# 384 rows of w4 moved to partitions 0 to 63 in eight-partition loads, and w3's products taken block by block

## The chip, the cores and the metric

The kernel runs on one core of a Trainium2 chip. The time is the device time of one execution in microseconds (us); the number that counts is the median of the runs, 197.53 us before the change.

## What is computed

One decode step (sequence length 1) of a small transformer block for a batch of 8 and a width D = 512, all in bf16:

```
A(x):  q = x @ wq  (32 heads of 128)                 k, v: the last 2048 positions of the caches (8 kv heads)
       softmax(q k^T / sqrt(128)) v, heads joined, @ wo
B(x):  x1 = x + hs          (the token shift is zero for a sequence of 1, so hs = 0)
       x1 + gelu(layernorm(x1) @ w3) @ w4            w3: 512 x 1792, w4: 1792 x 512
h   = x + A(layernorm(x))
out = h + B(layernorm(h))
```

The caches are the bulk of the work: 16 units of K and 16 of V of 2 MB each, against 4 MB each of `wq` and `wo` and 1.8 MB each of `w3` and `w4`.

## The kernel before

**Order and queues.** The program is written as five lists, one for each engine (`PE`, `AC`, `DV`, `PO`, `SP`; class `Engine`, line 47). Each entry names the semaphores that it waits for, and each engine works through its list in order. Nearly every transfer is issued by SyncE (`dma`, line 187), so all loads go through one queue, in the order in which they were written: `wq`, then K and V units as their buffers come free, `wo` in pieces, and last `w3` and `w4`. A load's semaphore rises by 16 in all as the DMA engines that carry it finish; a wait for 16 is a wait for the whole load.

**Attention.** For each K unit (lines 461 to 502) TensorE turns 128x128 blocks over (line 267), ScalarE and VectorE copy the result out (lines 273 and 275), and TensorE forms the scores (line 291). One softmax is done per batch row. V units follow three units later (line 372). The V unit that comes last is loaded in four pieces (line 415), and the last half of `wo` in four single groups (lines 513 and 514).

**The end, around the change.** TensorE multiplies the attention output by `wo` (line 433) into `hT_ps`, features on partitions and batch in the columns. VectorE takes the mean (lines 534 to 541, with a small TensorE product in line 537); `hb` (line 538) is the centred input to `w3`. A second small product (line 558) gives the variance; ScalarE takes the root (lines 559 and 560), VectorE the reciprocals (561, 562) and the residual `fin` (564).

`w3` (line 519) is loaded into the buffer of K unit 12 in four loads of 128 rows, under one semaphore. `w4` (lines 520 to 526) goes into the buffer of K unit 13 in four loads over all 128 partitions: three of 512 rows with four rows per partition (`w4_a`; 4 KB a partition) and one of 256 rows with two rows per partition (2 KB a partition). A chunk is what one product of `w4` contracts, 128 rows, one from each partition; there are FC = 14. Since a partition holds rows 4p to 4p+3 of its load, the matching columns of `w3` are picked with a stride of 4, or of 2 in the last load (`w3_cols`, line 546).

`pe_w3` (line 551) goes over the chunks and, in each, over the four blocks of 128 rows of `w3`, so each 128x8 result is finished before the next begins; it is called twice, for seven chunks each, and the first call waits for all of `w3` (line 565). Each half is scaled by VectorE (line 570) and put through the gelu by ScalarE (line 572). `pe_w4` (line 579) then adds the 14 chunks into one tile `z_ps`, with waits for the gelu halves and for the loads: the first waits for two loads of `w4` (`sem_w4a`), the others for `sem_w4b` and `sem_w4c`. Line 587 adds the residual, line 590 turns the result, line 591 copies it and line 594 stores it.

Of the kernel before, what the change touches and what calls it, by code (L numbers as in the profile page):

```python
# [7 lines left out]
ACT = mybir.ActivationFunctionType  # L8
ALU = mybir.AluOpType
AX = mybir.AxisListType  # L10

B = 8
D = 512
# [6 lines left out]
W0 = SK - W  # L20
NC = W // 128
F = 1792
FC = F // 128
KC = D // 128
EPS = 1e-5
GELU_C = math.sqrt(2.0 / math.pi)
# [4 lines left out]
U = 4  # L31
# [4 lines left out]
NK = 4  # L36
# [40 lines left out]
def bass_sequential_preLN__sliding_block_cached__mixer_s_mlp__decode_kernel(  # L77
# [19 lines left out]
    NUN = NB * NU  # L97
# [4 lines left out]
    with es:  # L102
        sb = lambda shape, dtype, name: es.enter_context(nc.sbuf_tensor(name, shape, dtype))
        ps_t = lambda shape, dtype, name: es.enter_context(nc.psum_tensor(name, shape, dtype))
        S = lambda name: es.enter_context(nc.semaphore(name))

        knat = sb([128, NK, UL], dt.bfloat16, "knat")
# [2 lines left out]
        wq_v = wbig[:, :].rearrange("p (k n) -> p k n", k=KC)  # L110
        wo_v = wbig[:, :].rearrange("p (g k n) -> p g k n", g=G, k=R)
        w3_sb = knat[:, 0, 0:KC * F].rearrange("p (k f) -> p k f", k=KC)
        w4_sb = knat[:, 1, 0:FC * D].rearrange("p (c n) -> p c n", c=FC)

        ident_f = sb([128, 128], dt.float32, "ident_f")
        ident_b = sb([128, 128], dt.bfloat16, "ident_b")
# [39 lines left out]
        at = [0]  # L156

        def tl(n, bf=False):
            t = tail[:, at[0]:at[0] + n]
            at[0] += n  # L160
            return t.bitcast(dt.bfloat16) if bf else t
        hs, hc, hsq, xb, fin = (tl(NH) for _ in range(5))
        hsum, vsum = tl(B), tl(B)
        vv, rr = tl(2 * B), tl(2 * B)
        g_x = tl(FC * B)
        hb, gT, fT = tl(NH // 2, True), tl(FC * B // 2, True), tl(NH // 2, True)
        out_sb = sb([NH, 128], dt.bfloat16, "out_sb")

        kT_ps = [ps_t([128, W], dt.bfloat16, f"kT_ps{i}") for i in range(2)]
        kbank = [kT_ps[i // 2][:, (i % 2) * 1024:(i % 2 + 1) * 1024].bitcast(dt.float32) for i in range(4)]  # L170
# [9 lines left out]
        sem_v = [S(f"sem_v{i}") for i in range(NV)]  # L180
        sem_vl = [S(f"sem_vl{i}") for i in range(U)]
        sem_wl = [S(f"sem_wl{i}") for i in range(2)]
        sem_x, sem_wq, sem_wo, sem_w3, sem_w4a, sem_w4b, sem_w4c, sem_out = (
            S(n) for n in ("sem_x", "sem_wq", "sem_wo", "sem_w3", "sem_w4a", "sem_w4b", "sem_w4c", "sem_out"))
        PE, AC, DV, PO, SP = (Engine(S(n)) for n in ("s_pe", "s_act", "s_dve", "s_pool", "s_sp"))

        def dma(eng, dst, src, sem, *waits):
            def f(e):
                e.dma_start(dst, src).then_inc(sem, 16)  # L189
            eng.op(f, *waits, inc=False)  # L190
# [16 lines left out]
        e = DV.op(lambda e: e.bn_stats(st6[:, :], x_sb[:, :]), X)  # L207
        e = DV.op(lambda e: e.bn_aggr(mv[:, :], st6[:, :]), e)
        e = AC.op(lambda e: e.activation(rstd[:, :], mv[:, 1:2], ACT.Sqrt, bias=eps1[0:B, :], scale=1.0), e, e_eps)
        e = DV.op(lambda e: e.reciprocal(rstd[:, :], rstd[:, :]), e)  # L210
# [24 lines left out]
        e = PE.op(pe_xT, e_xln, e_idb)  # L235
# [20 lines left out]
        e_T, e_Tlo, e_Thi, e_lo, e_hi, e_QK, e_PV = {}, [], [], [], [], {}, {}  # L256
        e_ev, e_Pz = {}, {}
        e_max, e_mT, e_neg, e_negps, e_negc, e_exp, e_PT, e_pS, e_lsel, e_Lb, e_rL, e_scale, e_sc = ({} for _ in range(13))
# [202 lines left out]
        for n in range(NUN):  # L461
# [8 lines left out]
            i = U * n  # L470
# [45 lines left out]
        e_gl = AC.op(lambda e: e.activation(scratch[:, 1:2], scratch[:, 0:1], ACT.Sqrt), e_warm)  # L516

        for k in range(KC):
            dma(SP, w3_sb[:, k, :], B_w3[128 * k:128 * (k + 1), :], sem_w3, e_T[U * (NUN - NK + 1) - 1])
        FA = 12  # L520
        w4_a = B_w4[0:FA * 128, :].rearrange("(a p c) n -> p a (c n)", p=128, c=4)
        for a, sem in ((0, sem_w4a), (1, sem_w4a), (2, sem_w4b)):
            dma(SP, w4_sb[:, 4 * a:4 * a + 4, :].rearrange("p c n -> p (c n)"), w4_a[:, a, :], sem,
                e_T[U * (NUN - NK + 2) - 1])
        dma(SP, w4_sb[:, FA:FC, :].rearrange("p c n -> p (c n)"),
            B_w4[FA * 128:F, :].rearrange("(p c) n -> p (c n)", c=FC - FA), sem_w4c)

        v3 = lambda t: t.rearrange("p (n b) -> p n b", b=B)
        vr = lambda t: t.rearrange("p (n b) -> p b n", b=B)

        def bc(a, k=KC):
            return bass.AP(tensor=a.tensor, offset=a.offset, ap=[a.ap[0], [0, k], [1, B]])
# [5 lines left out]
        e_hb = DV.op(lambda e: e.tensor_tensor(v3(hb[:, :]), v3(hs[:, :]), bc(st1), ALU.add), e_mu, e_hs)  # L538
        e = DV.op(lambda e: e.tensor_tensor(v3(hc[:, :]), v3(hs[:, :]), bc(st1), ALU.add))
        e = DV.op(lambda e: e.tensor_tensor(hsq[:, :], hc[:, :], hc[:, :], ALU.mult), e)  # L540
        e_vs = DV.op(lambda e: e.tensor_reduce(vsum[:, :], vr(hsq[:, :]), AX.X, ALU.add), e)

        y_ps = [kbank[0], kbank[2]]
        FH = FC // 2

        def w3_cols(kc, f):
            a, c = divmod(f, 4)
            s = 4 if a < 3 else 2
            return w3_sb[:, kc, 512 * a + c:512 * a + c + 127 * s + 1:s]

        def pe_w3(e, n, f0, f1):
            for f in range(f0, f1):
                for kc in range(KC):
                    ins = e.matmul(y_ps[n][:, f * B:(f + 1) * B], w3_cols(kc, n * FH + f),
                                   hb[:, kc * B:(kc + 1) * B], start=(kc == 0), stop=(kc == KC - 1))
            return ins

        e = PE.op(lambda e: e.matmul(st2, ones_v[:, :], vsum[:, :], start=True, stop=True), e_vs, e_sc[NUN - 1])  # L558
        e2 = AC.op(lambda e: e.activation(vv[:, 0:B], st2, ACT.Sqrt, bias=eps2[:, :], scale=1.0 + EPS), e)  # L559
        e1 = AC.op(lambda e: e.activation(vv[:, B:2 * B], st2, ACT.Sqrt, bias=eps1[:, :], scale=1.0))  # L560
        e_rr = DV.op(lambda e: e.reciprocal(rr[:, 0:B], vv[:, 0:B]), e2)
        e_r1 = DV.op(lambda e: e.reciprocal(rr[:, B:2 * B], vv[:, B:2 * B]), e1)
        e = DV.op(lambda e: e.tensor_tensor(v3(xb[:, :]), v3(hc[:, :]), bc(rr[:, B:2 * B]), ALU.mult), e_r1)
        e_fin = DV.op(lambda e: e.tensor_tensor(fin[:, :], hs[:, :], xb[:, :], ALU.add), e)
        e_y = [PE.op(lambda e: pe_w3(e, 0, 0, FH), e_hb, (sem_w3, 16 * KC), e_lo[-1], e_hi[-1], e_lo[-2], e_hi[-2]),
               PE.op(lambda e: pe_w3(e, 1, 0, FH))]
        e_gT = []
        for n in range(2):
            cs = slice(n * FH * B, (n + 1) * FH * B)
            e = DV.op(lambda e, n=n, cs=cs: e.tensor_tensor(v3(g_x[:, cs]), v3(y_ps[n][:, 0:FH * B]),  # L570
                                                            bc(rr[:, 0:B], FH), ALU.mult), e_y[n], e_rr)
            e_gT.append(AC.op(lambda e, cs=cs: e.activation(gT[:, cs], g_x[:, cs], ACT.Gelu_apprx_tanh), e))

        z_ps = S_ps[1]
        for lo, hi, waits in ((0, FH, (e_gT[0], e_exp[NB - 1], (sem_w4a, 32))),
                              (FH, 8, (e_gT[1],)),
                              (8, FA, ((sem_w4b, 16),)),
                              (FA, FC, ((sem_w4c, 16),))):
            def pe_w4(e, lo=lo, hi=hi):
                for fc in range(lo, hi):  # L580
                    for nb in range(KC):
                        ins = e.matmul(z_ps[:, nb * B:(nb + 1) * B], w4_sb[:, fc, nb * 128:(nb + 1) * 128],
                                       gT[:, fc * B:(fc + 1) * B], start=(fc == 0 and nb == 0),
                                       stop=(fc == FC - 1), skip_group_check=True)
                return ins
            e_z = PE.op(pe_w4, *waits)
        e = DV.op(lambda e: e.tensor_tensor(fT[:, :].rearrange("p (b n) -> p n b", n=KC), v3(fin[:, :]),
                                            v3(z_ps[:, 0:NH]), ALU.add), e_z, e_fin)
        o_ps = sm[0:NH, 64:128].bitcast(dt.bfloat16)
        e = PE.op(lambda e: e.matmul(o_ps, fT[:, :], ident_b[:, :], is_transpose=True), e)  # L590
# [40 lines left out]
```

## Time and profile before

| | |
|---|---|
| median of 3 runs | 197.53 us (197.46 to 197.57) |
| the profiled execution | 197.9 us, its span 196.5 us, so 1.4 us around the span |
| mean granted TensorE clock | 0.862 over the span; 0.50 in every stretch from 170 us on |
| busy share of the span | PE 81%, PEld 66%, DVE 51%, ACT 44%, POOL 2% |
| HBM read | 79.18 MB, 403 GB/s over the span |
| packets of the program's DMA queue | 96.0% of sixteen DMA engines' span; packets of kind "instruction" on a queue of their own: 23, 0.38 MB, 0.8% |

All times below are counted from the first instruction of the span. The trace holds one execution; its sum is therefore made against 197.9 us, which is 0.37 us above the median. Beside the instructions the trace has a record of every DMA packet (start, length, size and queue, but not which of the sixteen engines carried it) and of every step of a load's semaphore.

### The profile page before, as it was taken

The numbers are of one execution on the slowest core, as the hardware profiler recorded it, in microseconds if no ns is written. First come the engines' busy times: TensorE is split into PE (matmuls) and PEld (weight loads), VectorE is DVE, ScalarE is ACT, GpSimd is POOL, SyncE is SP. The second block draws the span as 40 slices with busy tenths as digits, with TensorE's granted clock in tenths as the row PEclk, the third lists the DMA queues.
The fourth block names the chain that finished last, engine by engine and source line by source line (L and its number), as shares of the span: only waits on it lengthen the run. The fifth ranks groups of instructions, "written<-read, shape, count | busy, mean of one in ns | idle before, by whom it ended". The sixth has DMA issues, their size and how long they took to land.

```text
span 196.5 us, 6336 instructions
## 1 busy us (share of the span) xinstructions
PE 159.3 (81%) x2925; PEld 130.0 (66%) x2925; DVE 100.0 (51%) x227; ACT 87.1 (44%) x100; POOL 4.4 (2%) x12
## 2 busy tenths in 40 slices
PE   0027986989998999999987699999999898887564
PEld 0027863766877677867765668697868585787463
DVE  7401445875484557558544375547554954720041
ACT  5000565864545454637453255545453673140030
POOL 8000000000000000000000000000000000000000
PEclk9999999999699969999999589957996998555555
DMA  6999999999999999999999999999999999999961
GB/s 228 440 417 430 434 430 434 427 425 420 420 419 425 424 424 424 420 429 427 417 420 427 424 427 427 430 424 427 427 424 429 420 424 427 400 408 406 408 269 42
DMA packets 7546, 79.59 MB, mean 405 GB/s; under 512 B 856, under 2 KB 864, under 8 KB 3424
## 3 DMA queue, kind: packets, MB, share of 16 engines
q1 hardware_dynamic: 7504, 79.18, 96.0%
q8 instruction: 23, 0.38, 0.8%
q14 instruction: 3, 0.02, 0.0%
q10 hardware_dynamic: 16, 0.01, 0.0%
HBM read 79.18 MB, written 0.01 MB: 403 GB/s over the span
## 4 chain that ended last, share of the span: by engine, by line
PE 46%; DMA 33%; DVE 13%; SPq 6%; issue 2%
PE kT_ps L267 30%; DMA knat<-in_A_k_cache_dram 26%; DMA knat<-in_B_w_dram 8%; PE S_ps L291 7%; SPq L189 6%; DVE kT_sb L275 5%; PE oT_ps L372 4%; DVE mcol L302 2%; DVE Pz L336 2%; PE sm L317 1%; PE sm L306 1%; DVE Mrow L308 1%; DVE rLk L356 1%; DVE rL L350 1%; DVE negrow L313 1%
## 5 line engine op out<-in xcount | busy, mean ns | idle before, releaser
L273 ACT ACTIVATE kT_sb<-kT_ps 128x1024 bf16<-128x1024 bf16 x64 | 65.0, 1023 | 48.2 <-PE kT_ps L267 47.7
L267 PE MATMUL kT_ps<-perm_k,knat 128*128 128x128 bf16 x1024 | 77.9, 238 | 4.0 <-DMA knat<-in_A_k_cache_dram 2.8
L267 PEld LDWEIGHTS kT_ps<-perm_k,knat 128*128 128x128 bf16 x1024 | 67.6, 108 | 11.5 <-issue 8.3
L275 DVE COPY kT_sb<-kT_ps 128x1024 bf16<-128x1024 bf16 x64 | 44.2, 690 | 38.4 <-PE kT_ps L267 38.2
L372 PEld LDWEIGHTS oT_ps<-pS,vnat 128*128 128x128 bf16 x1024 | 29.7, 98 | 8.3 <-issue 7.5
L372 PE MATMUL oT_ps<-pS,vnat 128*128 128x16 bf16 x1024 | 33.6, 171 | 2.0 <-DVE oK L382 0.9
L291 PE MATMUL S_ps<-kT_sb,qz 128*32 128x512 bf16 x256 | 26.5, 402 | 4.7 <-DVE kT_sb L275 4.2
L336 DVE TENSOR_TENSOR Pz<-P_sb,mJ 128x512 bf16<-128x512 bf16 x32 | 21.6, 682 | 0.0
L323 ACT ACTIVATE P_sb<-S_ps,negcol 128x512 bf16<-128x512 f32 x8 | 5.5, 687 | 23.4 <-DVE negcol L320 23.4
L291 PEld LDWEIGHTS S_ps<-kT_sb,qz 128*32 128x32 bf16 x256 | 7.1, 93 | 12.1 <-ACT kT_sb L273 4.1
L273 ACT ACTIVATE pS<-kT_ps 128x1024 bf16<-128x1024 bf16 x8 | 8.2, 1023 | 14.9 <-PE kT_ps L267 14.9
L275 DVE COPY pS<-kT_ps 128x1024 bf16<-128x1024 bf16 x8 | 5.5, 691 | 7.9 <-PE kT_ps L267 7.9
L382 DVE TENSOR_TENSOR oK<-oT_ps,rLk 128x64 bf16<-128x64 f32 x16 | 3.6, 224 | 11.4 <-PE oT_ps L372 11.4
L267 PE MATMUL kT_ps<-perm_p,Pz 128*128 128x128 bf16 x128 | 9.4, 231 | 0.0
L267 PEld LDWEIGHTS kT_ps<-perm_p,Pz 128*128 128x128 bf16 x128 | 8.1, 105 | 1.6 <-issue 1.6
L243 PE MATMUL S_ps<-xlnT,wbig 128*128 128x8 bf16 x128 | 3.6, 168 | 6.7 <-DMA wbig<-in_A_wq_dram 6.7
L243 PEld LDWEIGHTS S_ps<-xlnT,wbig 128*128 128x128 bf16 x128 | 3.5, 104 | 6.8 <-issue 6.8
L302 DVE TENSOR_REDUCE mcol<-S_ps 128x1 f32<-128x512 f32 x8 | 5.5, 691 | 4.8 <-PE S_ps L291 4.8
L559 ACT ACTIVATE Pz<-oT_ps,eps 128x8 f32<-128x8 f32 x1 | 0.3, 267 | 15.2 <-PE oT_ps L558 15.2
L250 DVE TENSOR_SCALAR qz<-S_ps 128x32 bf16<-128x32 f32 x8 | 0.9, 181 | 9.3 <-PE S_ps L243 9.3
L433 PE MATMUL S_ps<-o,wbig 128*128 128x8 bf16 x128 | 3.9, 168 | 2.1 <-issue 1.7
L231 PE MATMUL sm<-ident_b,xln_b 8*128 8x8 bf16 x4 | 0.3, 175 | 6.3 <-DVE xln_b L211 6.3
(78 smaller groups left out, 77.9 us busy)
## 6 DMA issues: line engine op xcount, KB each, us to landing
knat<-in_A_k_cache_dram SPq DMA_DIRECT2D x16, 2048.0 KB, 29.6
vnat<-in_A_v_cache_dram SPq DMA_DIRECT2D x15, 2048.0 KB, 31.8
wbig<-in_A_wq_dram SPq DMA_DIRECT2D x1, 4096.0 KB, 12.5
wbig<-in_A_wo_dram SPq DMA_DIRECT2D x2, 1024.0 KB, 31.6
vnat<-in_A_v_cache_dram SPq DMA_DIRECT2D x4, 512.0 KB, 10.3
wbig<-in_A_wo_dram SPq DMA_DIRECT2D x4, 512.0 KB, 11.2
knat<-in_B_w_dram SPq DMA_DIRECT2D x4, 448.0 KB, 12.5
knat<-in_B_w_dram SPq DMA_DIRECT2D x3, 512.0 KB, 14.5
```

Source lines behind the costliest of these rows:

```text
L189: e.dma_start(dst, src).then_inc(sem, 16)
L243: ins = e.matmul(S_ps[0][:, h * B:(h + 1) * B], wq_v[:, kc, h * DH:(h + 1) * DH], xlnT[:, kc * B:(kc + 1) * B], start=(kc == 0), stop=(kc ...
L267: ins = e.matmul(kT_ps[k % 2][:, c * 128:(c + 1) * 128], src[:, c * DH:(c + 1) * DH], perm[:, :], is_transpose=True)
L273: e_lo.append(AC.op(lambda e: e.activation(dst[:, 0:1024], kT_ps[k % 2][:, 0:1024], ACT.Copy), e_Tlo[k], *free))
L275: e_hi.append(DV.op(lambda e: e.tensor_copy(dst[:, 1024:2048], kT_ps[k % 2][:, 1024:2048]), e_Thi[k], *free))
L291: ins = e.matmul(S_ps[b % 2][32 * j:32 * (j + 1), :].rearrange("p (c r) -> p c r", c=16), qz[:, b, J * t + j, lo:lo + 32], kT_sb[:, i % NK ...
L302: e_max[b] = DV.op(lambda e: e.tensor_reduce(mcol[:, :], S_ps[b % 2][:, :], AX.X, ALU.max), e_QK[NU * U * (b + 1) - 1], e_mT.get(b - 1))
L323: e_exp[b] = AC.op(lambda e: e.activation(P_sb[:, :], S_ps[s][:, :], ACT.Exp, bias=negcol[:, s:s + 1], scale=1.0, accum_out=lcol[:, s:s + 1]),
L336: e_Pz[b, part] = DV.op(lambda e: e.tensor_tensor(Pz[:, 0, J * w * part:J * w * (part + 1)].rearrange("p (x j) -> p x j", j=J), p_bc, m_bc ...
L372: ins = e.matmul(dst, vnat[:, n % NV, (16 * w + c) * DH:(16 * w + c + 1) * DH], mvg, start=(w == 0 and c == 0), stop=(w == U - 1 and c == 15),
L382: e_sc[n] = DV.op(lambda e: e.tensor_tensor(oK[:, n % 2].rearrange("p g r k -> p (g r) k"), s_bc, rLk[:, b % 2, 16 * t:16 * t + 16, :], AL ...
L433: ins = e.matmul(hT_ps[:, nb * B:(nb + 1) * B], wo_v[:, g, k, nb * 128:(nb + 1) * 128], o2[:, g, k, :], start=False, stop=(g == G - 1 and ...
```

## The change

- `w4` has 11 chunks of 128 rows (FCM) and six chunks of 64 rows (FX), 17 in all. The last 384 rows lie six per partition on partitions 0 to 63 (`w4x_sb`), in the buffer of K unit 14. They come in eight loads of eight partitions each; the partitions of one load lie four apart, and each holds 6 KB. These eight loads stand in SyncE's queue between `w3` and the rest of `w4`.
- The other 1408 rows come in three loads over 128 partitions: two of 512 rows (four per partition), each now with a semaphore of its own, and one of 384 rows (three per partition).
- Each block of 128 rows of `w3` has a semaphore of its own. TensorE takes the blocks in the outer loop and all 17 chunks in the inner one, so a block's products wait for that block alone, and all results are finished in the last block. The results lie in three PSUM banks: six chunks of 64 rows, eight of 128, three of 128.
- The scaling and the gelu run in three parts, in that order, and so do the products with `w4`: the 64-row chunks first, then the others. There are 68 products with `w3` and 68 with `w4`; before there were 56 and 56.

```diff
-FC = F // 128
+FX = 6
+FCM = (F - 64 * FX) // 128
+FA = 8
+FC = FCM + FX
+FX0 = FCM * 128
...
+        w4x_sb = knat[0:64, 2, 0:FX * D].rearrange("p (c n) -> p c n", c=FX)
...
         for k in range(KC):
-            dma(SP, w3_sb[:, k, :], B_w3[128 * k:128 * (k + 1), :], sem_w3, e_T[U * (NUN - NK + 1) - 1])
-        FA = 12
+            dma(SP, w3_sb[:, k, :], B_w3[128 * k:128 * (k + 1), :], sem_w3[k], e_T[U * (NUN - NK + 1) - 1])
+        w4_x = B_w4[FX0:F, :].rearrange("(h a i c) n -> h i a (c n)", h=2, a=8, c=FX)
+        for h in range(2):
+            for i in range(4):
+                dma(SP, w4x_sb[32 * h + i:32 * h + i + 29:4, :, :].rearrange("p c n -> p (c n)"), w4_x[h, i], sem_w4x,
+                    e_T[U * (NUN - NK + 3) - 1])
...
-        for a, sem in ((0, sem_w4a), (1, sem_w4a), (2, sem_w4b)):
-            dma(SP, w4_sb[:, 4 * a:4 * a + 4, :].rearrange("p c n -> p (c n)"), w4_a[:, a, :], sem,
-                e_T[U * (NUN - NK + 2) - 1])
-        dma(SP, w4_sb[:, FA:FC, :].rearrange("p c n -> p (c n)"),
-            B_w4[FA * 128:F, :].rearrange("(p c) n -> p (c n)", c=FC - FA), sem_w4c)
+        for a in range(FA // 4):
+            dma(SP, w4_sb[:, 4 * a:4 * a + 4, :].rearrange("p c n -> p (c n)"), w4_a[:, a, :], sem_w4a[a], w4_free)
+        dma(SP, w4_sb[:, FA:FCM, :].rearrange("p c n -> p (c n)"),
+            B_w4[FA * 128:FX0, :].rearrange("(p c) n -> p (c n)", c=FCM - FA), sem_w4b)
...
+        parts = ((FCM, FC, 64, kbank[1]), (0, FA, 128, kbank[0]), (FA, FCM, 128, kbank[2]))
...
+        def pe_w3(e, kc, f0, f1, m, y):
             for f in range(f0, f1):
-                for kc in range(KC):
-                    ins = e.matmul(y_ps[n][:, f * B:(f + 1) * B], w3_cols(kc, n * FH + f),
-                                   hb[:, kc * B:(kc + 1) * B], start=(kc == 0), stop=(kc == KC - 1))
+                ins = e.matmul(y[0:m, (f - f0) * B:(f - f0 + 1) * B], w3_cols(kc, f), hb[:, kc * B:(kc + 1) * B],
+                               start=(kc == 0 and f == f0), stop=(kc == KC - 1), skip_group_check=True)
...
+        for kc in range(KC):
+            e_y = [PE.op(lambda e, kc=kc, p=p: pe_w3(e, kc, *p), e_hb, (sem_w3[kc], 16), *y_free) for p in parts]
...
+        for f0, f1, n, waits in ((FCM, FC, 0, ((sem_w4x, 128), e_exp[NB - 2])), (0, 4, 1, ((sem_w4a[0], 16),)),
+                                 (4, FA, 1, ((sem_w4a[1], 16),)), (FA, FCM, 2, ((sem_w4b, 16),))):
```

More of the change, by code (lines that the diff above doesn't have):

```diff
@@ L112, in bass_sequential_preLN__sliding_block_cached__mixer_s_mlp__decode_kernel @@
         w3_sb = knat[:, 0, 0:KC * F].rearrange("p (k f) -> p k f", k=KC)
-        w4_sb = knat[:, 1, 0:FC * D].rearrange("p (c n) -> p c n", c=FC)
+        w4_sb = knat[:, 1, 0:FCM * D].rearrange("p (c n) -> p c n", c=FCM)
+        w4x_sb = knat[0:64, 2, 0:FX * D].rearrange("p (c n) -> p c n", c=FX)
         ident_f = sb([128, 128], dt.float32, "ident_f")
@@ L182, in bass_sequential_preLN__sliding_block_cached__mixer_s_mlp__decode_kernel @@
         sem_wl = [S(f"sem_wl{i}") for i in range(2)]
-        sem_x, sem_wq, sem_wo, sem_w3, sem_w4a, sem_w4b, sem_w4c, sem_out = (
-            S(n) for n in ("sem_x", "sem_wq", "sem_wo", "sem_w3", "sem_w4a", "sem_w4b", "sem_w4c", "sem_out"))
+        sem_w3 = [S(f"sem_w3{i}") for i in range(KC)]
+        sem_w4a = [S(f"sem_w4a{i}") for i in range(2)]
+        sem_x, sem_wq, sem_wo, sem_w4b, sem_w4x, sem_out = (
+            S(n) for n in ("sem_x", "sem_wq", "sem_wo", "sem_w4b", "sem_w4x", "sem_out"))
         PE, AC, DV, PO, SP = (Engine(S(n)) for n in ("s_pe", "s_act", "s_dve", "s_pool", "s_sp"))
@@ L518, in bass_sequential_preLN__sliding_block_cached__mixer_s_mlp__decode_kernel @@
         for k in range(KC):
-            dma(SP, w3_sb[:, k, :], B_w3[128 * k:128 * (k + 1), :], sem_w3, e_T[U * (NUN - NK + 1) - 1])
-        FA = 12
-        w4_a = B_w4[0:FA * 128, :].rearrange("(a p c) n -> p a (c n)", p=128, c=4)
-        for a, sem in ((0, sem_w4a), (1, sem_w4a), (2, sem_w4b)):
-            dma(SP, w4_sb[:, 4 * a:4 * a + 4, :].rearrange("p c n -> p (c n)"), w4_a[:, a, :], sem,
-                e_T[U * (NUN - NK + 2) - 1])
-        dma(SP, w4_sb[:, FA:FC, :].rearrange("p c n -> p (c n)"),
-            B_w4[FA * 128:F, :].rearrange("(p c) n -> p (c n)", c=FC - FA), sem_w4c)
+            dma(SP, w3_sb[:, k, :], B_w3[128 * k:128 * (k + 1), :], sem_w3[k], e_T[U * (NUN - NK + 1) - 1])
[4 more added lines that the diff above has]
+                    e_T[U * (NUN - NK + 3) - 1])
+        w4_free = e_T[U * (NUN - NK + 2) - 1]
+        w4_a = B_w4[0:FA * 128, :].rearrange("(a p c) n -> p a (c n)", p=128, c=4)
+        for a in range(FA // 4):
+            dma(SP, w4_sb[:, 4 * a:4 * a + 4, :].rearrange("p c n -> p (c n)"), w4_a[:, a, :], sem_w4a[a], w4_free)
+        dma(SP, w4_sb[:, FA:FCM, :].rearrange("p c n -> p (c n)"),
+            B_w4[FA * 128:FX0, :].rearrange("(p c) n -> p (c n)", c=FCM - FA), sem_w4b)
         v3 = lambda t: t.rearrange("p (n b) -> p n b", b=B)
@@ L541, in bass_sequential_preLN__sliding_block_cached__mixer_s_mlp__decode_kernel @@
         e_vs = DV.op(lambda e: e.tensor_reduce(vsum[:, :], vr(hsq[:, :]), AX.X, ALU.add), e)
-        y_ps = [kbank[0], kbank[2]]
-        FH = FC // 2
+        parts = ((FCM, FC, 64, kbank[1]), (0, FA, 128, kbank[0]), (FA, FCM, 128, kbank[2]))
         def w3_cols(kc, f):
[L547 to L551, printed above, removed]
+            if f >= FCM:
+                at, st, m = FX0 + f - FCM, FX, 64
+            elif f >= FA:
+                at, st, m = FA * 128 + f - FA, FCM - FA, 128
+            else:
+                at, st, m = 512 * (f // 4) + f % 4, 4, 128
+            return w3_sb[:, kc, at:at + (m - 1) * st + 1:st]
+        def pe_w3(e, kc, f0, f1, m, y):
             for f in range(f0, f1):
-                for kc in range(KC):
-                    ins = e.matmul(y_ps[n][:, f * B:(f + 1) * B], w3_cols(kc, n * FH + f),
-                                   hb[:, kc * B:(kc + 1) * B], start=(kc == 0), stop=(kc == KC - 1))
+                ins = e.matmul(y[0:m, (f - f0) * B:(f - f0 + 1) * B], w3_cols(kc, f), hb[:, kc * B:(kc + 1) * B],
+                               start=(kc == 0 and f == f0), stop=(kc == KC - 1), skip_group_check=True)
             return ins
@@ L564, in bass_sequential_preLN__sliding_block_cached__mixer_s_mlp__decode_kernel @@
         e_fin = DV.op(lambda e: e.tensor_tensor(fin[:, :], hs[:, :], xb[:, :], ALU.add), e)
-        e_y = [PE.op(lambda e: pe_w3(e, 0, 0, FH), e_hb, (sem_w3, 16 * KC), e_lo[-1], e_hi[-1], e_lo[-2], e_hi[-2]),
-               PE.op(lambda e: pe_w3(e, 1, 0, FH))]
+        y_free = (e_lo[-1], e_hi[-1], e_lo[-2], e_hi[-2])
+        for kc in range(KC):
+            e_y = [PE.op(lambda e, kc=kc, p=p: pe_w3(e, kc, *p), e_hb, (sem_w3[kc], 16), *y_free) for p in parts]
         e_gT = []
[L568 to L572, printed above, removed]
@@ L574, in bass_sequential_preLN__sliding_block_cached__mixer_s_mlp__decode_kernel @@
-        z_ps = S_ps[1]
[L575 to L580, printed above, removed]
+        for n, (f0, f1, m, y) in enumerate(parts):
+            cs = slice(f0 * B, f1 * B)
+            e = DV.op(lambda e, m=m, y=y, cs=cs, k=f1 - f0: e.tensor_tensor(
+                v3(g_x[0:m, cs]), v3(y[0:m, 0:k * B]), bc(rr[0:m, 0:B], k), ALU.mult), e_y[n], e_rr)
+            e_gT.append(AC.op(lambda e, m=m, cs=cs: e.activation(gT[0:m, cs], g_x[0:m, cs], ACT.Gelu_apprx_tanh), e))
@@ L581, in pe_w4, with w4_of @@
+        z_ps = S_ps[1]
+        def w4_of(f, nb):
+            w = w4_sb[:, f] if f < FCM else w4x_sb[:, f - FCM]
+            return w[:, nb * 128:(nb + 1) * 128]
+        for f0, f1, n, waits in ((FCM, FC, 0, ((sem_w4x, 128), e_exp[NB - 2])), (0, 4, 1, ((sem_w4a[0], 16),)),
+                                 (4, FA, 1, ((sem_w4a[1], 16),)), (FA, FCM, 2, ((sem_w4b, 16),))):
+            def pe_w4(e, f0=f0, f1=f1, m=parts[n][2]):
+                for fc in range(f0, f1):
                     for nb in range(KC):
-                        ins = e.matmul(z_ps[:, nb * B:(nb + 1) * B], w4_sb[:, fc, nb * 128:(nb + 1) * 128],
-                                       gT[:, fc * B:(fc + 1) * B], start=(fc == 0 and nb == 0),
-                                       stop=(fc == FC - 1), skip_group_check=True)
+                        ins = e.matmul(z_ps[:, nb * B:(nb + 1) * B], w4_of(fc, nb), gT[0:m, fc * B:(fc + 1) * B],
+                                       start=(fc == FCM and nb == 0), stop=(fc == FCM - 1), skip_group_check=True)
@@ L585, in pe_w4 @@
                 return ins
-            e_z = PE.op(pe_w4, *waits)
+            e_z = PE.op(pe_w4, e_gT[n], *waits)
         e = DV.op(lambda e: e.tensor_tensor(fT[:, :].rearrange("p (b n) -> p n b", n=KC), v3(fin[:, :]),
```

## The prediction

> **What bounds the kernel now.** I read the page's DMA slices first, then the chain that ended last, then stretches of 2 us and the order of time over the end. The chain's last pieces (start, length, what):
>
> ```profile
> 177.90 15.19 DMA knat<-in_B_w_dram
> 193.10 0.05 issue
> 193.14 0.59 PE S_ps L582 x16
> 193.73 0.04 issue
> 193.78 0.39 PE S_ps L582 x8
> ```
>
> The third load of `w4` lands at 193.10, the fourth at 193.73, and TensorE stands between and before; the last product ends at 194.17. So the end hangs on a transfer. The stretches (the last two columns are the share of the sixteen DMA engines that was busy, and GB/s) show what kind of transfer:
>
> ```profile
> 186.00:188.00 2.00, 1.50 (x36) 1.31 (x33) 0.47 (x4) 0.00 (x0) 0.00 (x0) 0.50 1.02 404
> 188.00:190.00 2.00, 1.16 (x19) 1.07 (x20) 0.91 (x7) 0.73 (x3) 0.00 (x0) 0.50 0.63 244
> 190.00:192.00 2.00, 1.44 (x46) 1.38 (x44) 0.77 (x4) 1.48 (x3) 0.00 (x0) 0.50 0.44 177
> 192.00:194.00 2.00, 1.87 (x56) 1.69 (x56) 0.00 (x0) 0.00 (x0) 0.00 (x0) 0.50 0.20 70
> ```
>
> From 188 on the engines fall idle one by one while the last load still comes in. All sixteen carry the same bytes, so some are late. The trace's steps of the last load's semaphore say how late: seven at 188.56 to 188.94, one at 190.71, eight at 191.64 to 193.73. The packet records say why. On one DMA engine each packet starts 3 to 4 ns before the one ahead has ended, so the records fall into sixteen strings. The 23 packets of kind "instruction" (16 KB, about 1.1 us each) go round eight of these strings in turn, each costing about 1.35 us (its 1.1 and a slow packet after it); by the end each of those eight has carried two or three. These are the late eight.
>
> **What the end costs beside the transfer.** The order of time:
>
> ```profile
> 188.62 0.60 PE L558 MATMUL oT_ps<-Pz,ones_v 128*128 128x8 f32 x2 [0.84 <-DVE Pz L541]
> ...
> 189.44 1.98 PE L554 MATMUL kT_ps<-Pz,knat 128*128 128x8 bf16 x56 [0.22 <-DMA knat<-in_B_w_dram]
> ...
> 189.70 1.28 ACT L572 ACT_TABLE_LOAD   x1
> ...
> 191.00 0.25 ACT L572 ACTIVATE Pz<-Pz 128x56 bf16<-128x56 f32 x1
> 191.45 0.22 DVE L570 TENSOR_TENSOR Pz<-kT_ps,Pz 128x56 f32<-128x56 f32 x1 [0.66 <-PE kT_ps L554]
> 191.70 0.25 ACT L572 ACTIVATE Pz<-Pz 128x56 bf16<-128x56 f32 x1 [0.46 <-DVE Pz L570]
> ```
>
> `w3`'s products wait 0.22 for its last block, landed at 189.39. The gelu's table is in at 190.98, the first gelu done at 191.25; but `w4`'s first products start at 191.97, after their two loads (191.84). Starts of single products: 33 ns apart where `w3` is read with a stride of 4, 27 with a stride of 2, and 27 for `w4`.
>
> **The change, part by part.**
> *w3 block by block.* Three blocks are down before 188.6, the last at 189.39. TensorE can start when the product of line 558 is through: 189.1 (its second pass starts at 188.86, a pass takes 0.24) to 189.25; I take 189.15. There are 68 products: 32 with stride 4 at 33 ns, 12 with stride 3 between 27 and 33 (I take 30), 24 of 64 columns with stride 6, which no row shows: between 27 (the least gap of any single-tile product here) and 40; I take 27, half the columns being loaded. Sum 1.06 + 0.36 + 0.65 = 2.06, so the last starts at 191.2 and ends at 191.35 (191.65 at 40 ns). Block 3 is needed only at 190.7.
> *Three gelu parts.* The first result is finished by product 57, at about 191.0. VectorE 0.22 and ScalarE 0.25 with two handovers of 0.03 give the first gelu at 191.55, the others 191.9 and 192.2 (a gelu each 0.3). They are hidden behind 24 products, 191.6 to 192.25, and 32 more, to 193.1.
> *w4's products.* 68 x 27 ns = 1.84 from 191.6, with 0.17 for the last one's length: end at 193.6, if no load is waited for. The 12 + 12 extra products cost 0.65, and this is in the sum.
> *w4's loads.* A packet of 4 KB takes 155 ns on its string. Before, each DMA engine had 3 x 8 packets of 4 KB and 8 of 2 KB; now two times 8 of 4 KB and 8 of 3 KB, which is 24 KB or 0.93 us less; eight engines get 8 packets of 6 KB on top, 1.86 us and eight semaphore packets (9 ns each). The 8-row load of `x` shows how such a load falls: eight 1 KB packets in eight strings. [...]
> If the eight engines are the early ones, the late eight land all at 193.73 - 0.93 = 192.80, the early ones at 188.94 + 0.99 = 189.9 (190.71 + 0.99 = 191.7 for the one in between). The needs are: `w4x` 191.6, first load 192.25 (lands 190.6), second 192.7 (191.84, as the second did before), third 193.1 (192.80). Nothing waits; the margin of the last is 0.3.
> *Issues.* Eight more on SP's queue, between `w3` and `w4`. Its issues took 0.44 to 2.98 us there; eight cost 3.5 us (at 0.44) to 12 (at 1.5). The last issue ended at 181.4, so now 185 to 193. I take 185, as the early engines, which these go to, hold less; they reach `w4` at about 186, so this hides by 1 us only, and each us beyond would delay the early engines, which have 2.9 us in hand. K unit 14's buffer has been free since about 153.
> *Sum.* Last product 193.6 instead of 194.17: -0.57, the tail behind it unchanged. Profiled execution 197.9 - 0.57 = 197.33; median 197.53 - 0.57 = 196.96.
>
> **Rivals.**
> *The eight loads go to the late eight (slower).* Then the late engines get 0.99 more, not 0.93 less: all down at 193.73 + 0.99 = 194.72, 12 products and a restart (0.05 + 0.30 + 0.17) end at 195.25: +1.1, 198.6. It decides by which engines these are. [...]
> *The loads don't shift (no change).* They spread over sixteen, or an instruction packet falls on an engine's last `w4` packets (1.35 us; the next comes when TensorE passes into a new block of instructions). Landing at 193.73 again, then 12 products: 194.3, or 197.6.
> *TensorE waits for its own instructions (no change).* At 185.13 the order of time has
>
> ```profile
> 185.13 1.77 PE L433 MATMUL S_ps<-o,wbig 128*128 128x8 bf16 x61 [1.72 <-issue]
> ```
>
> a stop in the middle of one group, while an instruction packet ran from 182.63 to 183.74; work resumes 1.4 us after it. From there to a hiccup of 91 ns at `w4`'s 7th product are 128 products, thus 256 instructions, 16 KB. With 12 more products for `w3` that border comes at its 63rd, 191.05. The packet before it ran 188.89 to 189.98; with the same 1.4 the instructions are there at 191.4. A stop of 0.3 before the last five products costs 0.1, as `w4` waits for the gelu till 191.6 anyway. But were the packet 0.4 us later, the gain would be 0.2 smaller: 197.35. [...]
>
> **Numbers.** Forecast 0.58, loads on the late eight 0.28, no shift 0.07, instructions 0.07. What a measurement here can tell from no change is 0.2%, 0.40 us. The forecast's own range, 196.7 (0.25 more from narrower products and an earlier start) to 197.3 (40 ns products, a restart or two), is faster by more than that in 0.51 of its 0.58; the first rival is slower in 0.26 of 0.28; the others are mostly the same, with 0.01 faster and 0.05 slower. Faster 0.52, same 0.17, slower 0.31. The range runs from 196.7 to 198.7, across the first rival's price.
>
> **What would show it.** In the changed profile: the share of busy DMA engines in 188 to 190 up and in 192 to 194 down to almost nothing, the last `w4` load down at about 192.8, the chain's end carried by TensorE and the gelu, and no wait of line `pe_w4` on a DMA. If the last load lands at 194.5 or later with half the engines idle from 187, the late eight got the rows. An "issue" gap in `w3`'s products at about 191 would be the border. The forecast is wrong if these products run at 40 ns or more, or if SP's last issue comes after 187.

## The result and the profile after

The changed kernel takes 199.52 us (median of 6 runs, 198.41 to 200.0) against 197.50 us (197.36 to 197.9) of the kernel before in the same comparison: a ratio over all runs of 1.0091 (95% interval 1.0063 to 1.0119; the two medians alone give 1.0102), so it is slower, by about 1%. The forecast was 196.96 us with a range up to 198.7. The profiled execution took 199.64 us with a span of 198.3 us; before it was 197.9 and 196.5.

The chain of waits of the changed kernel, from the variance product on (start, length, what). Line 571 is the variance product, 567 the products with `w3`, 584 the scaling, 586 the gelu, 599 the products with `w4`:

```profile
188.90 0.59 PE oT_ps L571 x2
189.50 3.89 PE kT_ps L567 x57
193.38 0.02 issue
193.41 0.21 DVE Pz L584
193.62 0.02 issue
193.64 0.25 ACT Pz L586
193.89 0.05 issue
193.94 2.09 PE S_ps L599 x68
```

No transfer is left in it. Before, two DMA landings (193.10 and 193.73) carried the end; now TensorE carries it from 189.50 on, but for one scaling and one gelu (0.21 and 0.25), and 57 products with `w3` alone take 3.89 us. The order of time has the same pieces whole (start, length, engine, line, what, count, and in brackets the idle time ahead and what ended it):

```profile
175.90 6.11 SPq L196 DMA_DIRECT2D knat<-in_B_w_dram  x10
...
185.41 1.76 PE L440 MATMUL S_ps<-o,wbig 128*128 128x8 bf16 x61 [1.72 <-issue]
...
188.90 0.59 PE L571 MATMUL oT_ps<-Pz,ones_v 128*128 128x8 f32 x2 [0.85 <-DVE Pz L552]
...
189.43 4.39 PE L567 MATMUL kT_ps<-Pz,knat 128*64 128x8 bf16 x68
...
193.94 2.07 PE L599 MATMUL S_ps<-Pz,knat 64*128 64x8 bf16 x68
```

`w3` takes 4.39 us where it took 1.98 for 56 products before. `w4`'s 68 products run through in 2.07 us without a wait. The last one ends at 196.01, before (by the same view) at 194.15: +1.86 us, nearly all of it what the spans differ by (1.8). The third column of the stretches (busy time of TensorE with its count) shows how slowly `w3` goes; the last two are the share of busy DMA engines and GB/s:

```profile
186.00:188.00 2.00, 1.72 (x47) 1.59 (x43) 0.29 (x2) 0.00 (x0) 0.00 (x0) 0.50 0.98 390
188.00:190.00 2.00, 1.15 (x9) 1.07 (x8) 0.85 (x6) 0.45 (x3) 0.00 (x0) 0.50 0.76 303
190.00:192.00 2.00, 2.00 (x35) 1.93 (x34) 0.58 (x4) 1.26 (x1) 0.00 (x0) 0.50 0.44 171
192.00:194.00 2.00, 1.88 (x34) 1.74 (x34) 0.43 (x3) 0.24 (x1) 0.00 (x0) 0.50 0.08 28
```

In 190 to 192 TensorE is busy all the time and starts only 35 products, one every 57 ns; the clock is 0.50, as it was before. The transfers did move as the forecast's first sign asked (0.63 to 0.76 in 188 to 190, 0.20 to 0.08 in 192 to 194), but the end no longer hangs on them. The groups by shape say which of the `w3` products are dear (busy time, mean ns of one; PE is the product itself, PEld the load of its weights):

```profile
L567 PE MATMUL kT_ps<-Pz,knat 128*64 128x8 bf16 x24 | 2.8, 235 | 0.0
L567 PEld LDWEIGHTS kT_ps<-Pz,knat 128*64 128x64 bf16 x24 | 2.5, 183 | 0.1
L567 PE MATMUL kT_ps<-Pz,knat 128*128 128x8 bf16 x44 | 2.1, 175 | 0.0
L567 PEld LDWEIGHTS kT_ps<-Pz,knat 128*128 128x128 bf16 x44 | 1.7, 116 | 0.1
```

The same of the kernel before:

```profile
L554 PE MATMUL kT_ps<-Pz,knat 128*128 128x8 bf16 x56 | 2.0, 174 | 0.2 <-DMA knat<-in_B_w_dram 0.2
L554 PEld LDWEIGHTS kT_ps<-Pz,knat 128*128 128x128 bf16 x56 | 1.9, 116 | 0.3 <-DMA knat<-in_B_w_dram 0.3
```

The 24 products whose weights are 64 columns six apart load them in 183 ns each; a load of twice as many columns takes 116. The starts of single products say the same more sharply. In each block of `w3` the six narrow products start 89 to 91 ns apart, with 111 after the first of them and 164 at the change back to 128 columns: 0.635 us from the first of the six to the first wide one behind them, and 0.445 us for the other eleven.

### The profile page after: what moved, and what is told of

The parts are those of the page before. It is cut to its first block, busy times and chain, and to the rows that moved or that the text cites. A ratio compares the mean times of both kernels' runs of the same rounds, so it can differ in the third digit from the quotient of the medians.

```text
span 198.3 us, 6395 instructions
## 1 busy us (share of the span) xinstructions
PE 160.8 (81%) x2949; PEld 131.6 (66%) x2949; DVE 99.9 (50%) x228; ACT 87.2 (44%) x101; POOL 4.4 (2%) x12
## 4 chain that ended last, share of the span: by engine, by line
PE 53%; DMA 25%; DVE 16%; issue 4%; ACT 1%; SPq 0%; DVEq 0%
PE kT_ps L274 29%; DMA knat<-in_A_k_cache_dram 25%; PE S_ps L298 7%; PE oT_ps L379 7%; DVE kT_sb L282 6%; DVE Pz L343 4%; DVE mcol L309 2%; PE kT_ps L567 2%; PE S_ps L440 2%; PE sm L324 1%; PE sm L313 1%; PE S_ps L599 1%; DVE Mrow L315 1%; PE sm L399 1%; DVE rLk L363 1%
## 5 line engine op out<-in xcount | busy, mean ns | idle before, releaser
L274 PE MATMUL kT_ps<-perm_k,knat 128*128 128x128 bf16 x1024 | 77.0, 236 | 4.7 <-issue 3.1
L274 PEld LDWEIGHTS kT_ps<-perm_k,knat 128*128 128x128 bf16 x1024 | 66.7, 107 | 12.3 <-issue 10.2
```

What stands on the lines that cost most here:

```text
L274: ins = e.matmul(kT_ps[k % 2][:, c * 128:(c + 1) * 128], src[:, c * DH:(c + 1) * DH], perm[:, :], is_transpose=True)
```

## The experiments

Two theories stood for the 1.8 us. One: the narrow strided weight loads set the end, whatever the transfers do. The other: six-per-partition rows on eight engines delay the last loads, and slow products only hide it. Both could be true one behind the other, so the kernels take the products and the transfers apart. Line numbers are those of each kernel.

**The products alone, in three steps.** All three keep the changed kernel's transfers and alter only which elements of `w3` the 24 products of the 64-row chunks read, so that part of the result is formed from other columns; their number stays.

e1_stride1 reads 64 columns that lie side by side:

```
-                at, st, m = FX0 + f - FCM, FX, 64
+                at, st, m = FX0 + 64 * (f - FCM), 1, 64
```

> The changed kernel, with the 64-column weights of w3 read from 64 neighbouring columns instead of every sixth (the output is then that of other columns). Theory A (a weight load of 64 columns is slow whatever its stride): the 24 narrow products stay 89 to 91 ns apart, w3's products take 4.3 to 4.4 us, time 199.2 to 199.8. Theory B (a stride of six elements is what is slow): they go to 27 ns, w3's products take 2.6 us or less, time 197.0 to 197.8.

Measured: 198.39 us, ratio 1.0041 (1.0027 to 1.0056); neither theory alone is met. From the order of time:

```profile
188.24 3.49 PE L567 MATMUL kT_ps<-Pz,knat 128*64 128x8 bf16 x68
191.86 2.07 PE L599 MATMUL S_ps<-Pz,knat 64*128 64x8 bf16 x68
```

The narrow products are now 53 to 54 ns apart. That is 0.9 us less for `w3`, but each still takes twice the 27 ns that a full-width one takes: the stride is one part of the cost, the width another.

e2_cols128_stride6 keeps the stride of six and reads 128 columns (`y[0:m, ...]` becomes `y[:, ...]` in `pe_w3`):

```
-                at, st, m = FX0 + f - FCM, FX, 64
+                at, st, m = F - 768 + f - FCM, FX, 128
```

> The changed kernel, with the 24 narrow products of w3 given 128 columns, still every sixth column (the upper 64 results are not used, and the columns are others). Theory A (64 columns are slow, 128 fast): 27 to 45 ns apart, w3's products take 2.1 to 2.8 us, time 197.0 to 198.0. Theory B (the stride): 90 ns apart or up to 180, since twice the columns are read: w3's products 4.3 to 6.5 us, time 199.3 to 201.5.

Measured: 198.28 us, 1.0033 (1.0020 to 1.0046). The products are 45 to 48 ns apart, mostly 46 or 47, faster than with half as many columns, and `w3` takes 2.63 us, as the expectation's theory A has it, though the time lies above its range. Its order of time and its chain:

```profile
188.21 2.63 PE L567 MATMUL kT_ps<-Pz,knat 128*128 128x8 bf16 x68
...
192.94 0.59 PE L599 MATMUL S_ps<-Pz,knat 128*128 128x8 bf16 x16 [0.56 <-DMA knat<-in_B_w_dram]
193.97 0.46 PE L599 MATMUL S_ps<-Pz,knat 128*128 128x8 bf16 x12 [0.44 <-DMA knat<-in_B_w_dram]
```

```profile
181.64 12.19 DMA knat<-in_B_w_dram
193.84 0.14 issue
193.97 0.47 PE S_ps L599 x12
```

As soon as the products are quick, the last load is what ends last: it is down at 193.84. The second theory's effect lies right behind the first one's.

e3_cols128_stride3 reads 128 columns three apart (`FX0 + (f - FCM) % 3, 3, 128`, and `y[:, ...]` as in e2), which makes these products as cheap as I had put them.

> The changed kernel, with the 24 narrow products given 128 columns at a stride of three, which the other products already use (28 to 30 ns apart there; the columns are others). All theories on the products: 28 to 33 ns, w3's products 2.1 to 2.4 us instead of 4.4, so the forecast of the sum can be seen without its mis-sized term: last product of w4 near 193.9 on the changed kernel's clock (its part ahead of w3 was 0.28 us later than in the kernel before), time 197.0 to 197.5. If something else than these products made the change slower, the time stays above 198.

Measured: 198.26 us, 1.0027 (1.0015 to 1.0038); products 26 to 28 ns apart, once in each block 31. The price is about as expected and the time is not: by the expectation's last sentence something else slows the kernel too. Nine of its ten executions took 198.1 to 198.45 us and one took 197.24, and the profile is of that one:

```profile
189.07 2.06 PE L567 MATMUL kT_ps<-Pz,knat 128*128 128x8 bf16 x63
...
191.33 0.28 PE L567 MATMUL kT_ps<-Pz,knat 128*128 128x8 bf16 x5 [0.21 <-issue]
191.55 2.07 PE L599 MATMUL S_ps<-Pz,knat 64*128 64x8 bf16 x68
```

This is nearly the forecast's picture: `w3` in 2.06 and 0.28 us, the instruction border (where the prediction puts the start of TensorE's next block of instructions) after the 63rd product with a stop of 0.21, `w4` from 191.55 with no wait on a load, the last product done at 193.62. The last two landings in this trace are 191.85 and 192.79. So part of the forecast's gain exists (197.24 against a median of 197.59 of the kernel before), in one execution of ten. e3_again is the same kernel once more, to have a trace of an ordinary execution.

> A second look at the kernel with 128 columns at a stride of three, whose profiled execution took 197.24 and whose others took 198.1 to 198.45. Theory D: in an execution of 198.1 or more, the instruction packet at 188 to 189 falls on a string that also carries eight packets of 6 KB, that string ends at 193.3 to 193.6, and w4's last load is waited for; in the one of 197.24 it fell on a string without them. If the time is near 198.3 and that packet is on a string without 6 KB packets, the theory falls.

Measured: 198.22 us. Its order of time:

```profile
191.94 0.57 PE L599 MATMUL S_ps<-Pz,knat 128*128 128x8 bf16 x16 [0.36 <-DMA knat<-in_B_w_dram]
...
193.10 0.59 PE L599 MATMUL S_ps<-Pz,knat 128*128 128x8 bf16 x16 [0.60 <-DMA knat<-in_B_w_dram]
194.13 0.46 PE L599 MATMUL S_ps<-Pz,knat 128*128 128x8 bf16 x12 [0.44 <-DMA knat<-in_B_w_dram]
```

The last two landings are 193.06 and 194.00, 1.2 us later than in the other trace. The packet records, put into sixteen strings (one for each DMA engine, as in the prediction), show the difference. Eight strings carry eight 6 KB packets each (234 ns a packet): five that are early, the one in between, and two of those that carry instruction packets. In e3_again the last instruction packet (188.04) lies in one of these two, which ends at 193.52. In the first trace it came at 188.91, in a string that carries no 6 KB packets, which ends at 191.89; the two late strings with rows end at 191.98 and 192.31. e2's trace has the slow pattern too: its packet came at 187.88, the 6 KB packet right behind it took 645 ns instead of 234, and the last landing is 193.84. TensorE wasn't the late one: its products with `wo` began at 184.28 in e3_again and at 185.13 in the first trace. Three traces are few, and which string that packet takes in the other executions isn't known, so this is argued and not shown as the cause of the step from 197.24 to 198.2; its size fits.

**The order of `w3`'s products alone.** e4_blocks_only is the kernel before with one semaphore for each block of `w3` and the blocks in the outer loop:

```
-        e_y = [PE.op(lambda e: pe_w3(e, 0, 0, FH), e_hb, (sem_w3, 16 * KC), ...),
-               PE.op(lambda e: pe_w3(e, 1, 0, FH))]
+        for kc in range(KC):
+            e_y = [PE.op(lambda e, kc=kc, n=n: pe_w3(e, kc, n), e_hb, (sem_w3[kc], 16), *y_free) for n in range(2)]
```

> The kernel before with one part of the change alone: w3's products by blocks of 128 rows, a semaphore for each block; w4's loads, its chunks and its waits as before. Theory A and B alike (the order by blocks costs nothing): w3's products start 0.2 to 0.3 us earlier and take 2.0 us, and the end still waits for w4's last load at 193.7: time 197.3 to 197.6, same. A third theory, C (changing the block and the PSUM bank within the loop is what is slow): w3's products take over 2.5 us and the time rises by 0.3 us or more.

Measured: 197.42 us, 0.9994 (0.9985 to 1.0004), no difference, as expected of the first two theories.

```profile
189.39 1.94 PE L554 MATMUL kT_ps<-Pz,knat 128*128 128x8 bf16 x56
...
191.84 0.99 PE L583 MATMUL S_ps<-Pz,knat 128*128 128x8 bf16 x32 [0.52 <-DMA knat<-in_B_w_dram]
193.01 1.00 PE L583 MATMUL S_ps<-Pz,knat 128*128 128x8 bf16 x24 [0.17 <-DMA knat<-in_B_w_dram]
```

`w3` starts 0.45 us after the variance product instead of 0.82, and what is gained there is waited for again at `w4`'s loads. The order is not what costs, and by itself it brings nothing.

**The transfers alone.** e9_even_wide is e3 with the 384 rows in one load over all 128 partitions, 3 KB each, so that all sixteen engines get the same; the products read half their rows from elsewhere in the buffer. e11_even_narrow is the changed kernel with the same load and its own narrow products. In both:

```
-        for h in range(2):
-            for i in range(4):
-                dma(SP, w4x_sb[32 * h + i:32 * h + i + 29:4, :, :]..., w4_x[h, i], sem_w4x, ...)
+        dma(SP, knat[:, 2, 0:3 * D], B_w4[FX0:F, :].rearrange("(p c) n -> p (c n)", c=3), sem_w4x, ...)
```

> The run with 128 columns at a stride of three, with the 384 rows loaded as one load of 128 partitions, 3 KB each, so that all sixteen DMA engines carry the same and each writes its own partitions; the products still read 64 partitions (six chunks, so part of what they read is not these rows). The 24 extra products, three gelu parts and the order by blocks stay. Theory D (the eight loads hold the end because late engines carry some of them): the last load lands near 193.4 to 193.7 and the time falls from 198.3 to 197.2 to 197.6. Theory E (the extra products and parts): it stays at 198.0 to 198.5.

> The changed kernel with that same even load and its 64-column products at a stride of six. Theory A (these products alone set the end): 199.0 to 199.7 as in the changed kernel. If the eight loads had a part in its 2 us: 198.5 or less.

Measured: e9 197.70 us, 1.0013 (1.0004 to 1.0021); e11 199.14 us, 1.0074 (1.0059 to 1.0088). e11 meets its first range, e9 lies 0.1 us above its own. The end of e9, then `w3` and `w4` of e11, in the order of time:

```profile
193.88 0.46 PE L596 MATMUL S_ps<-Pz,knat 128*128 128x8 bf16 x12 [0.45 <-DMA knat<-in_B_w_dram]
```

```profile
189.20 4.37 PE L564 MATMUL kT_ps<-Pz,knat 128*64 128x8 bf16 x68
...
193.69 2.07 PE L596 MATMUL S_ps<-Pz,knat 64*128 64x8 bf16 x68
```

With the narrow products it makes no clear difference how the rows come: 1.0074 and the changed kernel's 1.0091 have intervals that overlap. Only the products differ between e11 and e9, on the same chip: 0.61% or 1.2 us. Between e3 and e9 only the loads differ: 0.14% by the ratios, 0.28 us, with overlapping intervals; e3_again's 198.22, on e9's chip, is above all ten runs of e9 (197.51 to 198.07). What is left in e9 (0.13%, 0.26 us) fits the end of its profiled execution: its last load is down at 193.75, as before, but 12 products follow it instead of 8, so the last one ends at 194.36 instead of 194.17.

**One load for the 64 partitions.** e6_one_load_narrow and e7_one_load_wide put the 384 rows on partitions 0 to 63 in a single load, which sixteen engines share. e6 has the changed kernel's products, e7 those of e3:

```
+        dma(SP, w4x_sb[:, :, :].rearrange("p c n -> p (c n)"), B_w4[FX0:F, :].rearrange("(p c) n -> p (c n)", c=FX), sem_w4x, ...)
```

> The changed kernel with its eight loads of eight partitions replaced by one load of the same 64 partitions, which spreads over all sixteen DMA engines; the 64-column products stay. If the narrow products set the end (theory A), the time stays at 199.0 to 199.8 although the bytes are even again. If the eight-partition loads are what is late (theory D), it falls to 197.5 to 198.5.

> The same one load, with the 24 products given 128 columns at a stride of three (the columns are others). Theory D (after the narrow products are out of the way, the two late DMA engines that also got rows of the eight-partition loads hold the end): the last load lands at 193.6 to 193.8 as in the kernel before, and the time falls from the 198.3 of the run with 128 columns and eight loads to 197.3 to 197.7. Theory E (the 24 extra products and three gelu parts are what is left): it stays at 198.0 to 198.5.

Measured: 200.60 us, 1.0158 (1.0135 to 1.0181), and 200.85 us, 1.0168 (1.0151 to 1.0184). Neither expectation was met. The stretches of e7:

```profile
184.00:186.00 2.00, 0.88 (x34) 0.88 (x34) 0.00 (x0) 0.00 (x0) 0.00 (x0) 0.50 1.01 249
186.00:188.00 2.00, 1.48 (x36) 1.30 (x32) 0.49 (x4) 0.00 (x0) 0.00 (x0) 0.50 1.05 354
188.00:190.00 2.00, 1.39 (x34) 1.39 (x35) 0.91 (x6) 0.74 (x3) 0.00 (x0) 0.50 0.99 224
```

The first of these in the kernel before:

```profile
184.00:186.00 2.00, 0.87 (x33) 0.86 (x33) 0.00 (x0) 0.00 (x0) 0.00 (x0) 0.50 1.03 409
```

The engines are busy all the time (1.01, 1.05, 0.99) and move 224 to 354 GB/s where busy engines moved 404 and 409 before: the packets themselves are slow. Those of 6 KB take 362 ns in the median and up to 692, against 234 in the changed kernel, and the last load is down at 196.70. The 3.5 KB packets of `w3` beside them take 271 ns in 184.0 to 184.5, against 140. So this load, which sixteen engines share, was slow on these 64 partitions, and the packets beside it were slow too: 249, 354 and 224 GB/s are 0.61, 0.87 and 0.55 of 409. Why, no run here shows. In the changed kernel's eight loads, which go to the same 64 partitions from eight engines, nothing of it is seen (234 ns a packet, 408 GB/s in 184 to 186).

**Loads of four partitions.** e8_four_partitions uses e3's products and sixteen loads of four partitions each (`"(j a i c) n -> j i a (c n)"`, j = 4, a = 4).

> 128 columns at a stride of three as before, and the 384 rows in sixteen loads of four partitions instead of eight loads of eight. [...]

Measured: 199.76 us, 1.0111 (1.0095 to 1.0127). 23 issues took 15.4 us of SyncE's queue, the last one ended at 186.6, and the 6 KB packets took up to 465 ns. Two costs came at once, late issues and slow packets, so the run doesn't tell which engines four partitions fall on. It is inconclusive.

**A smaller shift.** c4_small_shift is the whole kernel with both costs made smaller: only 256 rows on partitions 0 to 63, four per partition (`FX = 4`), 128 columns with a stride of 4 for each of their products (the upper 64 results are not used), and the last 512 rows of `w4` in two loads of two rows per partition, so that 8 products follow the last load.

> A whole kernel that computes everything: 256 rows instead of 384 on partitions 0 to 63 (four per partition, rows 1024 to 1279, so that 128 columns at a stride of four lie within a block and the upper 64 results are left unused), eight loads of eight partitions, the rest in two loads of 512 rows and two of 256. Theory D with a shift of 0.62 us each way: late engines without these rows down at 193.1, late ones with them at 193.1 to 193.6: time 197.1 to 197.7, same as before within 0.2%. If narrow weight loads and the stride of six were the whole of it: 196.9 to 197.2.

Measured: 197.96 us, 1.0014 (1.0003 to 1.0026), above both expected ranges. Three of twelve executions took 197.05 to 197.21, the others 197.84 to 198.16. The profile is of the one at 197.05:

```profile
188.26 2.42 PE L570 MATMUL kT_ps<-Pz,knat 128*128 128x8 bf16 x64
...
192.96 0.38 PE L603 MATMUL S_ps<-Pz,knat 128*128 128x8 bf16 x8 [0.19 <-DMA knat<-in_B_w_dram]
```

The two groups of times stand apart as e3's do. No version here is faster than the kernel before by more than its interval.

## Why the prediction was wrong

**The step that failed** is a term of the sum: "24 of 64 columns with stride 6, which no row shows: between 27 ... and 40; I take 27, half the columns being loaded". The 24 products cost 4 x 0.635 = 2.54 us and not 0.65, and with that the direction was wrong as well: the whole gain forecast was 0.57. From the first to the last start `w3` takes 4.22 us instead of 2.06, +2.16: 1.89 in these, and the rest in the first wide and the first narrow product after each change of width; the forecast's own condition ("wrong if these products run at 40 ns or more") came true at 90.

Two factors, 2.0 for the width and 1.7 for the stride, make 90 out of 27. The spacings that the runs show, in ns, all at a granted clock of 0.50:

| columns, apart | 1 | 2 | 3 | 4 | 6 |
|---|---|---|---|---|---|
| 128 columns | 27 | 27 | 26 to 31 | 33 | 45 to 48 |
| 64 columns | 53 to 54 | | | | 89 to 91 |

Half the columns cost twice as much, at a stride of 1 (53 against 27) and of 6 (90 against 47) alike, and a stride of 6 costs 1.7 times a stride of 1, at either width. "Half the columns being loaded" had the direction wrong. The trace of before had a hint of the stride's cost: 33 ns at a stride of 4 against 27 at 2. The upper end of 40 came from no row. What happens inside TensorE at a width or a stride no run here shows.

**How the rest of the sum fared.** `w3` began 0.53 us after the variance product, as forecast, against 0.82 before: the block order gave its 0.29, though e4 shows that this counts for nothing while loads set the end. `w4`'s products took 2.07 where 1.84 and 0.17 were put. The gelu parts behind the first were hidden. The eight issues took 0.62 to 0.77 us each and SyncE's last one ended at 182.0, not 185, so this cover was never at stake. The products with `wo` began 0.28 later than in the trace of before (185.41, 185.13), behind the same stop of 1.72, which ended 1.34 us after an instruction packet, before 1.39; over the traces of this study that start lies anywhere from 184.23 to 185.46, and for one kernel, e3's, at 185.13 and 184.28, so a step of 0.28 needs no cause in the change. The sum by these: 193.6 + 0.28 + 2.16 - 0.11 + 0.06 = 195.99, against 196.01 measured; the 0.11 is that `w4` followed `w3`'s last start by 0.29 instead of 0.40, and the 0.06 is 2.07 less 2.01.

**"If the eight engines are the early ones"** was the second wrong step, and the rival ("the late eight") was as wrong. No trace of before shows on which engines such loads fall; that they fall on the early ones was the author's assumption. The strings of the changed kernel show a mix: five early, the middle one, two late. The six late strings without rows end at 190.38 and at 191.60 to 191.91, the forecast's 0.93 gained. The two late ones with rows end at 192.22 and 193.45, the latter with an instruction packet at 189.07; the last landing is 193.93. In the changed kernel nobody waits for it, because `w3` is slower still. With quick products it is the end (193.84 in e2, 194.00 in e3_again). So with cheap products, as in e3, the change would still have been slower, by 0.27%: between my forecast and the rival's 198.6, and nearer the rival. e3's fast trace has its last landing at 192.79, the forecast's 192.80, but that is luck: it belongs to a late string with rows, which the forecast didn't have.

**The instruction border** was placed rightly: e3 stops after the 63rd product for 0.21 us, as the third rival has it, and e3_again and e9 for 0.20. In the changed kernel no stop shows there. The prediction's 256 instructions to 16 KB are an estimate, and the trace of before fits it: 23 packets of 16 KB for 5850 products and weight loads, about 254 to a packet. That the next packet comes when TensorE passes into a new block is inferred as well: in five traces the packet at 188 to 189 starts 3.6 to 3.8 us after TensorE resumes behind its stop (185.13 and 188.89 before, 185.41 and 189.07 after the change, 184.27 and 187.88 in e2, 185.13 and 188.91 in e3, 184.28 and 188.04 in e3_again).

**Where the 0.91% is,** by differences of ratios: 0.64 in the narrow strided weight loads (0.61 between e11 and e9), some 0.14 in rows on two late engines, 0.13 in the longer work behind the last load. The first is shown by two pairs of runs (the changed kernel and e3, e11 and e9); the split of the other two is within their intervals, and they show only once the products are quick.

## What to carry to other kernels

What a product cost here went with how its weights are read: before packing rows so that a product loads 64 columns, or columns many elements apart, look at how far apart such products start in a trace, because half the columns took twice the time (53 against 27, 90 against 47). Reading 128 columns at the same stride and leaving 64 results unused, as e2 does, cost half as much. A price that no row shows needs a bound that a row gives, and where the whole gain (0.57 us) is no larger than what 24 products cost more at 51 ns than at 27, that bound decides the sign. And when a transfer is to be moved to idle engines, make sure first which engines a load of so many partitions falls on; here, with quick products, a mix of early and late ones left a gain in one execution of ten.

## What was not expected of the hardware

- At a granted clock of 0.50, products whose weights are 64 columns started every 53 ns with the columns side by side and every 90 with the columns six apart; with 128 columns it was 27 and 47. The change from 128 to 64 columns and back cost more: 96 to 98 and 111 ns for the first two starts, 164 on the way back (97, 76 and 126 in e1).
- A load of eight partitions four apart ran its 6 KB packets at 234 ns each on eight engines that were neither all the early nor all the late ones (five early, one between, two late). A single load of 64 partitions over sixteen engines ran them at 362 ns in the median, and the rate with everything beside it was 224 to 354 GB/s.
- The same kernel (e3) took 197.24 us once and 198.1 to 198.45 otherwise, and in the two traces of it the difference goes with which of sixteen engines carries one instruction packet; that this is the cause is argued from these and one more trace.
